# Loading taps and the norm's gain as single rows spread by TensorE, and the first x with its halo in one row a partition

## The chip, the cores and the metric
The kernel runs on one core of a Trainium2 chip. The metric is device time in microseconds (us), the median of repeated runs. The core has five engines with programs of their own: TensorE (PE; PEld are its weight loads), VectorE (DVE), ScalarE (ACT), GpSimd (POOL) and SyncE (SP). SP, ACT and POOL issue transfers (DMA), which 16 shared DMA engines carry out.

## The reference
A causal convolution with 7 taps, one set of taps for each of 8 heads of 24 columns, is followed by a feed-forward block with a layer norm in front and a residual around it. `x` is 8 x 4224 x 192, and x, the taps and g (192 values) are float32; W1 (192 x 768) and W2 (768 x 192) are float64.

```python
w = np.exp(weight - np.max(weight, axis=-1, keepdims=True))     # [8, 7]
w = w / (np.sum(w, axis=-1, keepdims=True) + 1e-09)
x_pad = np.concatenate([zeros(B, 6, D), x], axis=1)
y = einsum('hk,bskhg->bshg', w, x_pad[:, idx].reshape(B, S, K, H, 24))
mu, var = mean(y), mean((y - mu) ** 2)                          # over the 192 columns
yn = (y - mu) / np.sqrt(var + 1e-06) * g_ln
out = y + np.maximum(yn @ w_ch1, 0.0) @ w_ch2
```

## The kernel before
Of each batch entry, 4096 rows are cut into 128 stretches of 32 rows, one stretch to a partition; the last 128 rows of all eight entries make a group of their own. Work goes group by group (`groups`, line 70). The first four groups are small: 6 rows of each stretch of entry 0, then 8 rows a partition of the leftovers, then 10 and 16 rows of entry 0. All later groups have 16. A group needs 6 rows more in front of its own, the halo. For the first group the partition's halo is the end of the stretch of the partition before it, and partition 0's halo is zero.

Per group the convolution runs on VectorE (`conv`, line 402), with the first tap on ScalarE (`first_tap`, line 374). The result y is transposed in 32 x 32 blocks, multiplied by W1 on TensorE (`up`, line 530, or `up_mixed`, line 589; matmuls at line 524), evicted with a ReLU by ScalarE, and multiplied by W2 (`down`, line 730, or `down_fast`, line 781). The mean is taken out by centring W1 once (`centre_w1`, line 326), and g is multiplied into W1's rows. Late groups use sums of quarters of the operands, so as to do fewer products.

The order of the work is written out by hand (`tc.manual_schedule()`); each engine runs its instructions in program order. This is the start, which the change touches:

- ACT issues three loads of g: `ga` (128 partitions, one 4-byte value each, line 192) and twice `gb` (64 partitions each, line 194). SP issues the taps, the same 224 bytes to each of 128 partitions (line 195), then W1 in three loads (lines 198 and 202), then x of the first group (`load_x(0)`: its body at line 163, its halo in two loads at line 165), then x of the second group in eight loads (line 139), then W2 (line 208).
- VectorE and ScalarE turn the taps into softmax weights (lines 255 to 264). ScalarE and POOL then build diagonal matrices of the taps for the last three heads (`tap_matrices`, line 310, and line 305), since the first group's last three heads are convolved on TensorE (`conv_on_pe`, line 315, matmuls at line 320).
- W1 comes as float64 words, which VectorE and ScalarE turn into float32 (`split_words` and `join_words`, lines 218 and 231). Two thirds of W1 go first (`words_a`), with `ga` as a factor at line 245, then the rest (`words_b`) with `gb`. ScalarE's share of `split_words` (lines 221 and 229) stands between two portions of `tap_matrices` (lines 364 to 366).
- TensorE's first work is 20 matmuls on constants whose result nobody reads (`keep_warm(20)`, line 925, matmuls at line 362). They need two constant tiles that POOL makes (lines 285 to 292). After them come the means of W1 (line 329), the first convolution matmuls (320), the rest of the means (332) and the other steps of `centre_w1` (344, 349); ScalarE copies the centred W1 out (354).
- VectorE starts the first group's convolution after `words_b`. W2 is turned into float32 after that.

PSUM is one tile of eight banks. `take_bank` hands them out in turn and `take_set` hands out four neighbours, 0 to 3 or 4 to 7. `carve` cuts short-lived tiles out of the room of the hidden activations. The semaphores that tell of landed loads rotate: a load waits before its issue until the load that used the same semaphore before it has landed. There are eight of them for SP and ACT together.

Of the kernel before, what the change touches and what calls it, by code (L numbers as in the profile page):

```python
# [7 lines left out]
F32 = mybir.dt.float32  # L8
# [3 lines left out]
ALU = mybir.AluOpType  # L12
AX = mybir.AxisListType
# [3 lines left out]
def kernel(  # L17
# [29 lines left out]
    nc = tc.nc  # L47
    PSUM = bass.MemoryType.PSUM
    B, S, D = x.shape
    H, K = weight.shape  # L50
    F = moe_w_ch1.shape[1]
    P = 128
    Q = 64
    C = 32
    GRP = D // H
    PAD = K - 1
    J = 16
    R = 2 * J
# [31 lines left out]
    xr = x[:, 0 : P * R].rearrange("b (p r) d -> b p (r d)", p=P)  # L90
# [12 lines left out]
    consts = ctx.enter_context(tc.tile_pool(name="consts", bufs=1))  # L103
# [15 lines left out]
    def take_bank():  # L119
        i = turn[0] % 8  # L120
        turn[0] = i + 1
        return all_banks[:, i]
# [9 lines left out]
    def load_x(g, queue=nc.sync):  # L132
        b, j0, n = groups[g]
        t = xpool.tile([P, J + PAD, D], F32, tag="xg", name=f"xg{g}")
        xg[g] = t
        flat = t.rearrange("p j d -> p (j d)")
        if b is None:
            for b in range(B):
                queue.dma_start(
                    out=flat[LP * b : LP * b + LP, 0 : (PAD + n) * D],  # L140
                    in_=bass.AP(
                        tensor=x.tensor, offset=(b * S + P * R - PAD) * D,
                        ap=[[n * D, LP], [1, (PAD + n) * D]],
                    ),
                )
            return
        if j0:
            queue.dma_start(
                out=flat[:, 0 : (n + PAD) * D], in_=xr[b, :, (j0 - PAD) * D : (j0 + n) * D]
            )  # L150
            return
        if b:

            queue.dma_start(
                out=flat[:, 0 : (PAD + n) * D],
                in_=bass.AP(
                    tensor=x.tensor, offset=(b * S - PAD) * D, ap=[[R * D, P], [1, (PAD + n) * D]]
                ),
            )
            nc.gpsimd.memset(t[0:1, 0:PAD, :], 0.0)  # L160
            return
        nc.gpsimd.memset(t[0:1, 0:PAD, :], 0.0)
        nc.sync.dma_start(out=flat[:, PAD * D : (PAD + n) * D], in_=xr[b, :, 0 : n * D])
        for p0, p1 in ((16, P), (1, 16)):
            nc.sync.dma_start(
                out=flat[p0:p1, 0 : PAD * D],
                in_=xr[b, p0 - 1 : p1 - 1, (R - PAD) * D : R * D],
            )

    taps = consts.tile([P, H, K], F32, name="taps")
    ga = consts.tile([P, 1], F32, name="ga")
    gb = consts.tile([P, 1], F32, name="gb")

    room = hpool.tile([P, NF * J * P], F32, tag="ht", name="room")
    taken = [0]
# [1 line left out]
    def carve(n, dtype):  # L180
        part = room[:, taken[0] : taken[0] + n].bitcast(dtype)
        taken[0] += n
        return part
# [3 lines left out]
    raw2 = raw2.rearrange("p (n w) -> p n w", w=2)  # L187
    w1_words = moe_w_ch1.bitcast(U32)
    w2_words = moe_w_ch2.bitcast(U32)
    g_col = moe_g_ln.rearrange("(d o) -> d o", o=1)  # L190

    nc.scalar.dma_start(out=ga, in_=g_col[0:P, :])
    for r in range(2):
        nc.scalar.dma_start(out=gb[Q * r : Q * r + Q, :], in_=g_col[P:D, :])
    nc.sync.dma_start(
        out=taps, in_=bass.AP(tensor=weight.tensor, offset=0, ap=[[0, P], [K, H], [1, K]])
    )
    nc.sync.dma_start(
        out=raw1[:, 0:2].rearrange("p s f w -> p (s f w)"), in_=w1_words[0:P, :]
    )  # L200
    for r in range(2):
        nc.sync.dma_start(
            out=raw1[Q * r : Q * r + Q, 2, :, :].rearrange("p f w -> p (f w)"),
            in_=w1_words[P:D, 2 * FH * r : 2 * FH * (r + 1)],
        )
    load_x(0)
    load_x(1)
    nc.sync.dma_start(
        out=raw2.rearrange("p (c d) w -> p c (d w)", d=D),
        in_=w2_words.rearrange("(c p) d -> p c d", p=P),  # L210
# [20 lines left out]
    def join_words(dst, raw, mant, power, g=None):  # L231
# [20 lines left out]
    raw1b = raw1[:, 2]  # L252
    wmax = consts.tile([P, H], F32, name="wmax")
    wsum = consts.tile([P, H], F32, name="wsum")
    nc.vector.tensor_reduce(wmax, taps, axis=AX.X, op=ALU.max)
    nc.vector.tensor_tensor(
        taps, taps, wmax.unsqueeze(2).to_broadcast([P, H, K]), op=ALU.subtract
    )
    nc.scalar.activation(taps, taps, AF.Exp)
    nc.vector.tensor_reduce(wsum, taps, axis=AX.X, op=ALU.add)  # L260
    nc.vector.tensor_scalar(wsum, wsum, scalar1=1e-9, scalar2=None, op0=ALU.add)
    nc.vector.reciprocal(wsum, wsum)
# [23 lines left out]
    for q in range(NQ):  # L286
        m = copy[C * q : C * q + C].rearrange("p (q i) -> p q i", q=NQ)
        nc.gpsimd.affine_select(
            out=m, in_=m, pattern=[[0, NQ], [-1, C]],
# [10 lines left out]
        out=unit, in_=unit, pattern=[[-1, P]], compare_op=ALU.not_equal, fill=1.0, base=0,  # L300
# [5 lines left out]
        out=diag[:, H - 1 - PE_HEADS[0]], in_=taps[:, H - 1, :].unsqueeze(2).to_broadcast([P, K, P]),  # L306
# [642 lines left out]
    for g in range(NG):  # L949
        mixed, last = g in MIXED, g + 1 == NG  # L950
        if g + 2 < NG:
            load_x(g + 2)
# [74 lines left out]
```

## Time and profile before

| what | us |
|---|---|
| median of 3 runs | 966.1 (965.45 to 967.09) |
| profiled execution | 964.65 |
| its span, first to last instruction | 962.8 |
| first tap load to first convolution matmul (line 320) | 0.80 to 16.16 |
| start of the first up-projection (line 524) | 27.35 |
| TensorE busy | 950.3 |
| VectorE busy | 897.2 |

The page of the profile gives busy time by engine, the chain of work that ended last, groups of instructions by source line with their idle time and what ended it, and transfers with their size and the time from issue to landing. The timeline lists instructions in order of time; `x40` says that 40 of one kind are merged, and brackets hold the idle time before the first one and what ended it. A matmul in float32 leaves two records. `room` is the tile that `carve` cuts from, and `ps` is PSUM. The 1.85 us between the profiled execution's time and its span lie before the first instruction or after the last one.

### The profile page before, as it was taken

How to read it: one execution, taken by the hardware profiler on the slowest of the kernel's cores; microseconds unless marked ns; L12 is line 12 of the kernel's file. 1: busy time of each engine (PE TensorE's matmuls, PEld its weight loads, DVE VectorE, ACT ScalarE, POOL GpSimd, SP SyncE). 2: the span in 40 equal slices, each digit the busy share in tenths (PEclk: the TensorE clock that was granted, in tenths of full speed). 3: DMA queues.
4: the chain of work that ended last, by engine and by line, in shares of the span. 5: the costliest groups of instructions: out<-in, count | busy, mean ns of one | idle time of the engine just before them, and what ended most of it. 6: DMA issues, size and time to landing. Idle time of an engine off the chain costs nothing.

```text
span 962.8 us, 38387 instructions
## 1 busy us (share of the span) xinstructions
PE 950.3 (99%) x17274; PEld 717.0 (74%) x17274; DVE 897.2 (93%) x1505; ACT 680.9 (71%) x1097; POOL 249.4 (26%) x383
## 2 busy tenths in 40 slices
PE   7999999999999999999999999999999999999997
PEld 6886586776859677686968778685867868586787
DVE  6999998999999999999999999989989999999867
ACT  5724669586787959687795968778695877866361
POOL 2004411612125131422116131341215221161300
PEclk9999999999999999999999999999999999999999
DMA  8343787769787786969688796968779696766031
GB/s 194 105 125 133 162 212 187 183 130 282 142 243 158 211 189 135 265 133 261 138 237 168 172 240 120 276 140 235 158 179 228 116 282 140 177 138 124 3 68 68
DMA packets 26386, 165.15 MB, mean 172 GB/s; under 512 B 3567, under 2 KB 4463, under 8 KB 18542
## 3 DMA queue, kind: packets, MB, share of 16 engines
q0 software_dynamic: 19120, 99.36, 52.7%
q1 hardware_dynamic: 6798, 63.34, 17.8%
q8 instruction: 135, 2.21, 0.9%
q14 instruction: 29, 0.24, 0.1%
q10 hardware_dynamic: 304, 0.00, 0.0%
HBM read 38.95 MB, written 50.33 MB: 93 GB/s over the span
## 4 chain that ended last, share of the span: by engine, by line
PE 96%; DMA 2%; DVE 2%; issue 0%; DVEq 0%
PE ps L524 48%; PE ps L798 41%; PE ps L745 6%; DMA xg<-in_x_dram 1%; DVE room L765 1%; PE ps L320 1%; DVE room L626 0%; DMA ga<-in_moe_g_ln_dram 0%; PE ps L344 0%; PE ps L349 0%; DVE y L890 0%; PE ps L332 0%; DVE room L774 0%; DVE ot L915 0%; DVE ot L900 0%
## 5 line engine op out<-in xcount | busy, mean ns | idle before, releaser
L408 DVE SCALAR_TENSOR_TENSOR y<-xg,taps,y 128x384 f32<-128x384 f32 (+3 forms) x734 | 367.2, 576 | 1.2 <-ACT y L383 0.5
L798 PE MATMUL ps<-room,w2sums 128*32 128x256 f32 (+1 forms) x4320 | 236.2, 375 | 0.2
L524 PE MATMUL ps<-yt,w 32*128 32x256 f32 (+2 forms) x4104 | 235.6, 379 | 0.1
L620 ACT COPY room<-ps 128x1024 f32<-128x1024 f32 (+1 forms) x132 | 172.0, 1303 | 78.7 <-PE ps L524 78.6
L524 PEld LDWEIGHTS ps<-yt,w 32*128 32x128 f32 x4104 | 204.9, 185 | 26.1 <-issue 9.1
L798 PEld LDWEIGHTS ps<-room,w2sums 128*32 128x32 f32 x4320 | 137.8, 110 | 93.4 <-ACT room L633 5.5
L798 PE MATMUL ps<-room,w 128*32 128x256 f32 (+1 forms) x3240 | 180.5, 375 | 0.1
L765 DVE TENSOR_TENSOR room<-room 128x1024 f32<-128x1024 f32 (+1 forms) x135 | 151.0, 1190 | 6.4 <-PE ps L798 6.4
L798 PEld LDWEIGHTS ps<-room,w 128*32 128x32 f32 x3240 | 103.9, 110 | 69.1 <-DVE room L626 5.2
L524 PE MATMUL ps<-ysums,w1sums 32*128 32x256 f32 x2160 | 125.2, 379 | 0.1
L524 PEld LDWEIGHTS ps<-ysums,w1sums 32*128 32x128 f32 x2160 | 109.0, 185 | 11.2 <-ACT room L620 3.7
L804 ACT COPY cs<-ps 128x256 f32<-128x256 f32 (+1 forms) x180 | 66.4, 370 | 44.1 <-PE ps L798 44.1
L633 ACT ACTIVATE room<-room 128x1024 f32<-128x1024 f32 (+1 forms) x74 | 90.7, 1249 | 8.1 <-DMA room<-parts_cs 7.3
L876 ACT ACTIVATE ot<-ot,r 128x192 f32<-128x192 f32 x232 | 93.8, 462 | 0.0
L883 POOL DMA_DIRECT2D out_dram<-ot x40 | 34.3, 1083 | 201.9 <-ACT ot L876 125.5
L383 ACT ACTIVATE y<-xg,taps 128x384 f32<-128x384 f32 (+3 forms) x141 | 72.8, 611 | 8.1 <-DMA out_dram<-y 6.9
L626 DVE TENSOR_TENSOR room<-room,ps 128x2048 f32<-128x2048 f32 (+1 forms) x20 | 42.5, 2127 | 34.9 <-PE ps L524 34.7
L439 DVE BATCH_NORM_STATS2 st<-y 128x6 f32<-128x192 f32 x264 | 70.2, 343 | 0.0
L524 PE MATMUL ps<-yt,w1sums 32*128 32x256 f32 x1080 | 65.1, 380 | 0.0
L804 ACT COPY room<-ps 128x256 f32<-128x256 f32 (+1 forms) x90 | 33.7, 375 | 44.3 <-PE ps L798 30.9
L524 PE MATMUL ps<-ysums,w 32*128 32x256 f32 x1080 | 64.6, 376 | 0.0
L394 ACT ACTIVATE tb<-xg,taps 128x384 f32<-128x384 f32 x112 | 62.0, 639 | 0.0
(104 smaller groups left out, 880.2 us busy)
## 6 DMA issues: line engine op xcount, KB each, us to landing
xg<-in_x_dram SPq DMA_DIRECT2D x15, 2112.0 KB, 18.1
out_dram<-ot POOLq DMA_DIRECT2D x29, 768.0 KB, 8.7
y<-tb POOLq DMA_DIRECT2D x28, 768.0 KB, 10.7
room<-room POOLq DMA_DIRECT2D x42, 512.0 KB, 5.1
out_dram<-y SPq DMA_DIRECT2D x13, 1536.0 KB, 9.7
room<-parts_cs POOLq DMA_DIRECT2D x14, 1024.0 KB, 7.7
room<-parts_tb POOLq DMA_DIRECT2D x14, 1024.0 KB, 7.5
xg<-in_x_dram SPq DMA_DIRECT2D x1, 1536.0 KB, 7.7
```

The lines of the kernel that those rows point to most:

```text
L383: nc.scalar.mul(y[g][:, 0:n, cs], xg[g][:, 0:n, cs], taps[:, h, 0:1])
L394: nc.scalar.mul(tb[g][:, 0:n, cs], xg[g][:, 1 : 1 + n, cs], taps[:, h, 1:2])
L408: nc.vector.scalar_tensor_tensor(out=y[g][:, 0:n, cs], in0=t[:, k : k + n, cs], scalar=taps[:, h, k : k + 1], in1=y[g][:, 0:n, cs], op0=AL ...
L439: nc.vector.bn_stats(out=sums[g][:, j, :], in_=y[g][:, j, :])
L524: nc.tensor.matmul(banks[:, q, i * w : i * w + w], right[rows, c, P * i : P * i + P], left[rows, :, c, :], start=(first and c == 0 and i = ...
L620: nc.scalar.activation(dst, src, AF.Relu) if relu else nc.scalar.copy(dst, src)
L633: nc.scalar.activation(c, c, AF.Relu)
L745: nc.tensor.matmul(bank[C * q : C * q + C, 0:w], w2[:, f, C * c : C * c + C], left, start=(f == 0), stop=(f == NF - 1),)
L765: nc.vector.tensor_tensor(a[:, *dst, f], a[:, *left, f], a[:, *right, f], op=op)
L798: nc.tensor.matmul(dst[C * q : C * q + C, 0:w], right[:, f, C * c : C * c + C], left[:, f, q], start=(first and f == PAIR), stop=(f == PAI ...
L804: nc.scalar.copy(to[:, c], dst[:, 0:w].rearrange("p (j t) -> p j t", t=t))
L876: nc.scalar.mul(ots[g][:, j, :], ots[g][:, j, :], rstd[g][:, j : j + 1])
```

## The change
The taps and g each come as one row of one partition. A matmul with a row of ones as weights copies the row of taps to all 128 partitions of a PSUM bank. Two more matmuls, each with 128 values of g as weights and a single one as the moving operand, turn g into two columns: its first 128 values, and its last 64 values twice over (for which g's tail is loaded once more behind the row). The softmax of the taps reads PSUM at its first two steps. ScalarE copies the two columns of g out to `gs`, between the taps' exponential and the first `tap_matrices`. The new bank is the first that `take_bank` hands out, and the three matmuls come first in TensorE's program.

The first group's x is no longer loaded as body and halo. Partitions 16 to 127 and partitions 1 to 15 each get one contiguous run of 12 rows (9216 bytes) in one load, and partition 0 gets its 6 own rows in a third. The loads of taps and g move to ACT's queue, three as before; SP's queue has one load less.

```diff
         nc.gpsimd.memset(t[0:1, 0:PAD, :], 0.0)
-        nc.sync.dma_start(out=flat[:, PAD * D : (PAD + n) * D], in_=xr[b, :, 0 : n * D])
         for p0, p1 in ((16, P), (1, 16)):
             nc.sync.dma_start(
-                out=flat[p0:p1, 0 : PAD * D],
-                in_=xr[b, p0 - 1 : p1 - 1, (R - PAD) * D : R * D],
-            )
+                out=flat[p0:p1, 0 : (PAD + n) * D],
+                in_=bass.AP(
+                    tensor=x.tensor, offset=(b * S + p0 * R - PAD) * D,
+                    ap=[[R * D, p1 - p0], [1, (PAD + n) * D]],
+                ),
+            )
+        nc.sync.dma_start(out=flat[0:1, PAD * D : (PAD + n) * D], in_=xr[b, 0:1, 0 : n * D])
...
-    ga = consts.tile([P, 1], F32, name="ga")
-    gb = consts.tile([P, 1], F32, name="gb")
+    gs = consts.tile([P, 2], F32, name="gs")
+    ga, gb = gs[:, 0:1], gs[:, 1:2]
...
-    g_col = moe_g_ln.rearrange("(d o) -> d o", o=1)
-
-    nc.scalar.dma_start(out=ga, in_=g_col[0:P, :])
+    row, ones = carve(H * K + 2 * P, F32)[0:1], carve(P, F32)[0:1]
+    g_row = row[:, H * K :]
+    nc.scalar.dma_start(out=row[:, 0 : H * K], in_=weight.rearrange("(o h) k -> o (h k)", o=1))
+    g_in = moe_g_ln.rearrange("(o d) -> o d", o=1)
+    nc.scalar.dma_start(out=g_row[:, 0:D], in_=g_in)
+    nc.scalar.dma_start(out=g_row[:, D : 2 * P], in_=g_in[:, P:D])
+    nc.vector.memset(ones, 1.0)
+    spread = take_bank()
+    nc.tensor.matmul(spread[:, 0 : H * K], ones, row[:, 0 : H * K], start=True, stop=True)
     for r in range(2):
-        nc.scalar.dma_start(out=gb[Q * r : Q * r + Q, :], in_=g_col[P:D, :])
-    nc.sync.dma_start(
-        out=taps, in_=bass.AP(tensor=weight.tensor, offset=0, ap=[[0, P], [K, H], [1, K]])
-    )
+        nc.tensor.matmul(
+            spread[:, H * K + r : H * K + r + 1], g_row[:, P * r : P * r + P], ones[:, 0:1],
+            start=True, stop=True,
+        )
+    raw_taps = spread[:, 0 : H * K].rearrange("p (h k) -> p h k", k=K)
...
-    nc.vector.tensor_reduce(wmax, taps, axis=AX.X, op=ALU.max)
+    nc.vector.tensor_reduce(wmax, raw_taps, axis=AX.X, op=ALU.max)
     nc.vector.tensor_tensor(
-        taps, taps, wmax.unsqueeze(2).to_broadcast([P, H, K]), op=ALU.subtract
+        taps, raw_taps, wmax.unsqueeze(2).to_broadcast([P, H, K]), op=ALU.subtract
     )
     nc.scalar.activation(taps, taps, AF.Exp)
+    nc.scalar.copy(gs, spread[:, H * K : H * K + 2])
```

## The prediction
> **What bounds the kernel now.** I read the engine shares and the chain that ended last on the page first, then the chain of the first 80 us in order of time, then the timeline of the first 50 us, then the waits.
>
> The page, engine shares:
> ```profile
> span 962.8 us, 38387 instructions
> ...
> PE 950.3 (99%) x17274; PEld 717.0 (74%) x17274; DVE 897.2 (93%) x1505; ACT 680.9 (71%) x1097; POOL 249.4 (26%) x383
> ```
> TensorE is busy for 99%. By stages it is busy 779.8 of the 780.0 us from 120 to 900 us, so nothing the change touches can be gained there. What can move is when TensorE's unbroken stream starts. The chain of the first 80 us (start, length, what):
> ```profile
> 0.80 4.46 DMA ga<-in_moe_g_ln_dram
> ...
> 5.27 10.80 DMA xg<-in_x_dram
> ...
> 16.16 1.95 PE ps L320 x14
> ...
> 27.35 13.13 PE ps L524 x285
> ...
> 52.32 15.75 PE ps L524 x288
> ```
> It says that g's first load releases the halo of x, the halo releases the first convolution matmul at 16.16, and from 27.35 on TensorE doesn't stop. I don't take the first arrow at its word. The halo's issue did wait for `ga` (a semaphore in rotation), but it was issued at 5.27 while the body of x, issued at 2.92, landed only at 13.0: the rings were full, and the wait cost nothing.
>
> The timeline, what sets 16.16:
> ```profile
> 4.88 7.68 PE L362 MATMUL ps<-room 128*128 128x128 f32 x40 [4.88 <-POOL room L292]
> ...
> 5.11 0.21 DVE L255 TENSOR_REDUCE wmax<-taps 128x8 f32<-128x56 f32 x1 [4.18 <-DMA taps<-in_weight_dram]
> ...
> 6.90 1.86 ACT L313 ACTIVATE room<-room,taps 128x128 f32<-128x128 f32 x6 [1.04 <-DVE taps L263]
> ...
> 8.68 0.56 DVE L220 TENSOR_SCALAR room<-room 128x768 uint32<-128x768 uint32 x1 [1.88 <-DMA room<-in_moe_w_ch_dram]
> ...
> 13.37 1.56 PE L329 MATMUL ps<-room 128*128 128x384 f32 x4 [0.81 <-DVE room L245]
> ...
> 15.52 0.62 DVE L245 SCALAR_TENSOR_TENSOR room<-room,gb 128x384 f32<-128x384 f32 x1
> ...
> 16.16 1.95 PE L320 MATMUL ps<-xg,room 128*128 128x144 f32 x14 [1.24 <-DMA xg<-in_x_dram]
> ...
> 16.60 6.81 DVE L408 SCALAR_TENSOR_TENSOR y<-xg,taps,y 128x144 f32<-128x144 f32 x24 [0.46 <-ACT y L383]
> ```
> Three things arrive together. x is complete at 16.07. VectorE is done with W1 at 15.52+0.62=16.14. TensorE has been free since 14.92. TensorE idles 0.81 us before L329 and 1.24 us before L320: 2.05 us to be had from it, no more. The keep-warm matmuls (L362) end at 12.56 and are covered today, because L329 waits for W1 until 13.37.
>
> The page and the first 60 us, transfers (KB each, us to landing):
> ```profile
> xg<-in_x_dram SPq DMA_DIRECT2D x1, 576.0 KB, 10.1
> ...
> room<-in_moe_w_ch_dram SPq DMA_DIRECT2D x2, 192.0 KB, 8.3
> ...
> gb<-in_moe_g_ln_dram ACTq DMA_DIRECT2D x2, 0.2 KB, 8.1
> ...
> ga<-in_moe_g_ln_dram ACTq DMA_DIRECT2D x1, 0.5 KB, 4.5
> ```
> Each 256-byte copy of `gb` takes about 8.1 us. The last one lands at 10.31.
>
> **What the Trainium skill says.** "DMA: Bandwidth & Descriptors", section Queues, rings and completion order: each engine takes turns between the queues that have work, a packet of descriptors at a time. The trace agrees, more coarsely: in its packet records the earliest engine writes the completion of W1's first load at 5.39 and its first `gb` packet starts at 5.40. A small load on ACT's queue waits for a whole transfer of SP's. The section Why a DMA increments its semaphore by 16 and not by 1 says that the slowest dimension fixes how many engines are used (127 rows: one; 112: sixteen; 15: fifteen). It fits the split of x at partition 16; no row here shows 127. "TensorE: Matmul & The Clock Gate", Part 1 (The HAM clock gate): the clock rises after a whole busy window of a free-running 3.4 us grid. Here the keep-warm records stand 0.213 us apart up to 11.0 us and 0.112 after, 6.1 us after their start. With the page's grid that delay is 3.4 to 6.8 us, so the 40 records take an estimated 6.1 to 7.7 us, middle 6.9.
>
> **The change, part by part.**
>
> *Loads.* The taps' 128 packets of 224 B, all from one address, start from 1.96 to 4.74; eight engines have them by 3.31, the other eight land up to 5.09. This lag of some 2 us stays with those engines up to x (body 10.33 to 13.0, halo 12.35 to 16.07). Without them W1's first load starts on all engines at about 2.0 (issue 0.80 instead of 1.24, first packet 1.16 after the first issue now). 48 KB an engine at the 22 GB/s that the records show (seven 6144 B packets from 3.77 to 5.74) is 2.2 us, plus a first latency: done at 4.5, not 8.65. Its two halves take 1.35 us each at most on the earliest engine now (5.43 to 6.77), 0.9 if faster: 6.3 to 7.2.
>
> *x.* The same 1147 KB in half as many packets. At 233 GB/s (the mean of the slices from 4.5 to 16.1 us) 4.9 us: landed at about 12, 15 if the lag of the engines had another cause. Not slower by the larger packets: 1536 KB of 12288 B landed in 7.7 us, latency included. SP issues one load fewer, so what follows is issued 0.44 earlier; POOL's program is not passed by anything. The one-row rest waits for the taps' row to land before it is issued (the semaphores rotate over eight loads), which the full rings hide; with empty rings it would cost one small landing, about 2 us. The second group's x follows, and W2's load behind it (26.65 now, needed at 27.30) moves with them.
>
> *Spread.* Three row loads on ACT's queue (three issues, as now), a memset (L216's kind, 0.06), three small matmuls, a PSUM reduce in L255's place (0.21). The taps' chain from landing to finished taps is 5.09 to 6.80 = 1.7 us; add 0.5 for the matmul (the first keep-warm record took 0.58 cold). These matmuls stand **ahead of the keep-warm matmuls** in TensorE's program, and the new copy of g on ACT stands ahead of L313. So both now wait for the landing G of the last piece of g. TensorE: keep-warm starts at G+0.4 (two records 0.21 apart), not at 4.88. ACT: L313 starts at G+0.75 (0.4, and a copy of L324's kind, 0.28), not at 6.90.
>
> *G.* By turns: if the taps' row gets ahead of W1's first load, g's two pieces come after W1's first load and its first half: 5.8 to 6.3. If it doesn't, they come a half later: 6.7 to 7.5. Bounds: nothing queued ahead, 3.8 (third issue at about 1.8, 1.16 to the first packet, some 0.8 to land); as late as `gb` now, 10.31. I take 6.7.
>
> *The sum on TensorE.* Keep-warm 7.1 to 14.0. L329 at 14.0. W1's first part is ready for it earlier, at 13.35: L313 starts at 7.45, its six take 1.80 until L221 may start, L221 to L245 takes 3.03 (9.27 to 12.30), L245 to L329 1.07. L320 1.40 later (13.37 to 14.76 is when it could have started now): 15.4, x being there since 12. Against 16.16 this is 0.76 earlier. One `take_bank` more shifts the banks by one: the first up-projection needs ScalarE's copies 2 to 5 of L354 instead of 3 to 6, 0.37 apart, so 0.37 earlier. Together 1.1 us.
>
> *VectorE beside it.* from L221's start to the end of W1 it is 6.87 (9.27 to 16.14), so W1 is done at 7.45+1.80+6.87=16.1, and the convolution starts there, 0.5 before today's 16.60 (ScalarE's first taps, free of x's wait, are then done before). It may lag TensorE by its idle 0.82 before L234 of W2 and by 0.3 (transposed at 51.95, L524 at 52.25); 0.5+1.1=1.6 covers the 1.1. After 68 us the reserve is about 10 us.
>
> The profiled execution took 964.65 with a span of 962.8; the median is 966.1. A gain of 1.1 makes the span 961.7 and the median **965.0**. A measurement can tell about 0.2%, 1.9 us; the forecast lies inside.
>
> **Rivals.**
> *All of it arrives (963.7).* g lands by 5.3, or the clock rises early: L329 at its covered 12.6, all 2.05 us of TensorE's idle time and the 0.37 are won: 2.4. For it: 2.05 us of idle time exist, and the rows are a few packets. Against: today's `gb` alternates with W1. From G=5.9 on (at the middle clock) the gain is under 1.9.
> *Keep-warm behind g (968.4, slower).* One mechanism: the last piece of g still lands about as late as `gb` now (10.1). Keep-warm 10.5 to 17.4, L320 18.8, 2.6 late, less 0.37: 2.3 lost. It decides from G=7.8 on (16.53 less 1.4, 6.9 and 0.4), by 0.2% from G=9.8. For it: the 8.1 us of `gb`. Against: W1 and its halves start some 2 us earlier.
> *Nothing arrives (966.3).* The lag of eight engines isn't the taps' doing. Then W1's first load lands only its 0.44 earlier, at 8.2, g's last piece with it at about 8.0, keep-warm ends at 15.3, and L320 starts at 16.7: 0.5 late, less 0.37. For it: the lag shows in `ga` too (3.03 to 5.26). Against: `ga` also reads one small address range, and later loads show no lagging half.
>
> **How the numbers follow.** Forecast 0.46, all arrives 0.31, slower 0.11, nothing 0.12. Faster by over 0.2%: 0.31 and 0.05 of the forecast's early edge, 0.36; slower: 0.10 (0.01 of the rival stays under 0.2%); within: 0.54. The range takes the full gain with run-to-run play (963.5), and at the other end G=8.3 with the slow clock: 966.9. The forecast's own range is 964.2 to 966.0 (G 5.9 to 7.5).
>
> **What would show it.** Right: L362 starts at 6.5 to 7.5, released by a matmul that waited for a g load; no idle time before L320 from x; x landed by 13; TensorE idle before L329 small; L524 at 26.0 to 26.5 and its second block some 1.1 us before 52.32. Wrong: L362 still at 4.9 (the full gain); x landing after 15 (the lag isn't the taps'); L362 after 8 (slower); the copy of g waiting on ACT beyond 8.3 with VectorE, not TensorE, late at L524; or a gain of L524 at 27.35 that is gone at 52.32.

## The result and the profile after

The median after is 965.7 us (964.37 to 967.42 over 22 runs), against 967.33 us (965.24 to 970.3 over 22 runs) of the kernel before, run beside it on the same chip. The ratio is 0.9981, with a 95% interval of 0.9973 to 0.9989: 1.84 us faster by the ratio. The interval leaves out 1, so the kernel is faster, but the gain stays just under the 0.2% (1.9 us) that the forecast took as the least a measurement can tell. The forecast was a gain of 1.1 us, and the range 963.5 to 966.9 holds the time.

The page of the kernel after, engine shares:
```profile
span 962.9 us, 38399 instructions
...
PE 950.6 (99%) x17280; PEld 716.5 (74%) x17280; DVE 897.8 (93%) x1506; ACT 681.0 (71%) x1098; POOL 249.8 (26%) x383
```
The profiled execution took 964.68 us. Its span is 962.9 us and that of before was 962.8, so the two pages show no gain at all while the medians do. One reason is the execution that was profiled before: its 964.65 us are less than any of the other 22 times of that kernel. A second profiled execution of the unchanged kernel, shown below, starts its stream 3.9 us later. The gain has to be looked for against that one too.

The timeline of the kernel after, start in us, length, engine and line, out<-in, and in brackets the idle time before it and what ended it:
```profile
2.14 0.64 PE L203 MATMUL ps<-room 1*128 1x56 f32 x2 [2.14 <-DMA room<-in_weight_dram]
...
6.72 0.58 PE L205 MATMUL ps<-room 1*128 1x1 f32 x2 [0.38 <-DMA room<-in_moe_g_ln_dram]
...
7.24 6.50 PE L376 MATMUL ps<-room 128*128 128x128 f32 x40
7.34 0.22 DVE L268 TENSOR_REDUCE wmax<-ps 128x8 f32<-128x56 f32 x1 [6.29 <-PE ps L205]
...
8.00 0.14 ACT L273 COPY gs<-ps 128x2 f32<-128x2 f32 x1
...
9.13 1.86 ACT L327 ACTIVATE room<-room,taps 128x128 f32<-128x128 f32 x6 [0.99 <-DVE taps L277]
...
14.70 1.56 PE L343 MATMUL ps<-room 128*128 128x384 f32 x4 [0.96 <-DVE room L258]
...
16.09 1.88 PE L334 MATMUL ps<-xg,room 128*128 128x144 f32 x14
...
16.85 0.62 DVE L258 SCALAR_TENSOR_TENSOR room<-room,gs 128x384 f32<-128x384 f32 x1
17.39 6.78 DVE L422 SCALAR_TENSOR_TENSOR y<-xg,taps,y 128x144 f32<-128x144 f32 x24
```
(L203 and L205 are the new matmuls, L376 is the keep-warm of the old L362, L343 and L334 are the old L329 and L320, L268 the old L255, L327 the old L313, L258 the old L245, L422 the old L408.) The row of taps is spread at 2.14, but VectorE's reduce of it waits until 7.34, and the releaser is not the spread of the taps (L203). It is the spread of g (L205). The tap matrices therefore start at 9.13, later than the 6.90 of before, and VectorE ends W1 at 17.47 and starts its convolution at 17.39, 0.8 later than before.

The chain that ended last, first 80 us of the kernel after (start, length, what):
```profile
1.58 5.10 DMA room<-in_moe_g_ln_dram
...
7.34 0.23 DVE wmax L268
...
9.13 1.86 ACT room L327 x6
...
14.70 1.56 PE ps L343 x4
16.25 1.72 PE ps L334 x14
```
Where the chain of before ran through x, it now runs through the last piece of g, the softmax of the taps, the tap matrices and W1. x is not in it.

The transfers of the first 60 us, kernel after (KB each, us from issue to landing):
```profile
xg<-in_x_dram SPq DMA_DIRECT2D x1, 1008.0 KB, 12.2
...
room<-in_moe_w_ch_dram SPq DMA_DIRECT2D x1, 768.0 KB, 5.9
...
xg<-in_x_dram SPq DMA_DIRECT2D x1, 135.0 KB, 12.4
```
W1's first load was issued at 0.80 and landed at 6.7 (8.65 before): the first of the 16 engines had its share at 4.4, the eighth at 4.9, the last at 6.7. The two loads of x were issued from 2.46 on; the second landed at 15.4.

TensorE's timeline where the stream begins, kernel after:
```profile
27.00 5.13 PE L538 MATMUL ps<-yt,w 32*128 32x192 f32 x96
32.29 8.43 PE L538 MATMUL ps<-yt,w 32*128 32x192 f32 x192 [0.15 <-ACT room L528]
40.65 11.91 PE L759 MATMUL ps<-room,w 128*32 128x192 f32 x288
52.48 1.79 PE L538 MATMUL ps<-yt,w 32*128 32x256 f32 x28
```
The same of the kernel before:
```profile
40.41 11.91 PE L745 MATMUL ps<-room,w 128*32 128x192 f32 x288
52.25 2.01 PE L524 MATMUL ps<-yt,w 32*128 32x256 f32 x32
```
A lead of 0.35 us at the first up-projection (27.00 against 27.35) is 0.23 us of lag at the second. It is lost within the first block, where ScalarE empties the PSUM banks (`room L528`) only after its share of W2's conversion, and VectorE, later than before, starts W2 at 28.07 instead of 27.30:
```profile
30.28 1.26 ACT L242 ACTIVATE spare<-spare,low 128x1152 int32<-128x1152 int32 x1 [0.16 <-DVE spare L239]
31.44 0.79 ACT L528 ACTIVATE room<-ps 128x768 f32<-128x768 f32 x1
```

### The profile page after: what moved, and what is told of

Read it like the earlier page. It is cut to its first block, busy times and chain, and to the rows that moved or that the text cites. A ratio compares the mean times of both kernels' runs of the same rounds, so it can differ in the third digit from the quotient of the medians.

```text
span 962.9 us, 38399 instructions
## 1 busy us (share of the span) xinstructions
PE 950.6 (99%) x17280; PEld 716.5 (74%) x17280; DVE 897.8 (93%) x1506; ACT 681.0 (71%) x1098; POOL 249.8 (26%) x383
## 4 chain that ended last, share of the span: by engine, by line
PE 96%; DVE 2%; DMA 1%; ACT 1%; issue 0%; ACTq 0%; DVEq 0%
PE ps L538 48%; PE ps L812 41%; PE ps L759 6%; DVE room L779 1%; PE ps L334 1%; DMA room<-in_moe_g_ln_dram 1%; DVE room L640 0%; DMA out_dram<-y 0%; ACT room L327 0%; PE ps L358 0%; DVE y L904 0%; PE ps L343 0%; ACT w L368 0%; PE ps L363 0%; PE ps L346 0%
## 5 line engine op out<-in xcount | busy, mean ns | idle before, releaser
L422 DVE SCALAR_TENSOR_TENSOR y<-xg,taps,y 128x384 f32<-128x384 f32 (+3 forms) x734 | 367.2, 577 | 0.2
L538 PEld LDWEIGHTS ps<-yt,w 32*128 32x128 f32 x4104 | 204.9, 185 | 26.5 <-issue 9.6
L408 ACT ACTIVATE tb<-xg,taps 128x384 f32<-128x384 f32 x112 | 61.8, 633 | 0.0
```

The lines of the kernel that those rows point to most:

```text
L408: nc.scalar.mul(tb[g][:, 0:n, cs], xg[g][:, 1 : 1 + n, cs], taps[:, h, 1:2])
L422: nc.vector.scalar_tensor_tensor(out=y[g][:, 0:n, cs], in0=t[:, k : k + n, cs], scalar=taps[:, h, k : k + 1], in1=y[g][:, 0:n, cs], op0=AL ...
L538: nc.tensor.matmul(banks[:, q, i * w : i * w + w], right[rows, c, P * i : P * i + P], left[rows, :, c, :], start=(first and c == 0 and i = ...
```

## The experiments

The theory after the result: the repeated read of the 224 bytes of taps delays half of the DMA engines; to be rid of it is worth several microseconds, and the change gives most of that back by what it makes wait for g. The rivals: the gain comes from the new load of x, or from fewer transfers in general, or there is nothing to be had beyond what the change shows. Where a number of DMA packets, of single engines or of the TensorE clock is given without a line of a view, it was read from the trace's own records. Times are medians; each ratio is to the kernel before run beside it, with its 95% interval.

### The two parts alone
`rows_only`: the kernel after, with x loaded as before.
```diff
+        nc.sync.dma_start(out=flat[:, PAD * D : (PAD + n) * D], in_=xr[b, :, 0 : n * D])
         for p0, p1 in ((16, P), (1, 16)):
             nc.sync.dma_start(
-                out=flat[p0:p1, 0 : (PAD + n) * D],
+                out=flat[p0:p1, 0 : PAD * D],
+                in_=xr[b, p0 - 1 : p1 - 1, (R - PAD) * D : R * D],
...
-        nc.sync.dma_start(out=flat[0:1, PAD * D : (PAD + n) * D], in_=xr[b, 0:1, 0 : n * D])
```


> Taps and g as rows, x of the first group still as body and halo. Theory (the broadcast load of the taps and the 256 four-byte loads of g make half of the DMA engines late, and without them W1 and x land earlier and more evenly): W1's first load lands at about 6.7 us as with the whole change, x by about 15, VectorE's first convolution at about 17.4 because it waits behind g; time 1.2 to 2.0 us under the kernel before, as the whole change. Rival (the half as many and larger packets of x bring the gain): the time is that of the kernel before within 0.5 us.

Measured: 965.46 us, 0.9976 (0.9967 to 0.9986), as the whole change within the intervals. `x_only` is the reverse, the kernel before with the new load of x:
```diff
-        nc.sync.dma_start(out=flat[:, PAD * D : (PAD + n) * D], in_=xr[b, :, 0 : n * D])
         for p0, p1 in ((16, P), (1, 16)):
             nc.sync.dma_start(
-                out=flat[p0:p1, 0 : PAD * D],
-                in_=xr[b, p0 - 1 : p1 - 1, (R - PAD) * D : R * D],
+                out=flat[p0:p1, 0 : (PAD + n) * D],
...
+        nc.sync.dma_start(out=flat[0:1, PAD * D : (PAD + n) * D], in_=xr[b, 0:1, 0 : n * D])
```


> Only the x load of the first group is changed; taps and g are loaded as in the kernel before. Theory (the gain is in the small loads): W1's first load lands at 8.2 to 8.7 us, x at about 16, the first convolution matmul within 0.3 us of 16.16, time within 0.5 us of the kernel before. Rival (the larger packets of x bring the gain): x lands 1 to 2 us earlier and the time is 1.2 to 2.0 us under the kernel before.

Measured: 969.22 us, 1.0018 (1.0009 to 1.0027): 1.7 us slower. Its timeline:
```profile
9.75 0.56 DVE L223 TENSOR_SCALAR room<-room 128x768 uint32<-128x768 uint32 x1 [2.76 <-DMA room<-in_moe_w_ch_dram]
...
19.28 2.88 PE L323 MATMUL ps<-xg,room 128*128 128x144 f32 x14 [3.27 <-DMA xg<-in_x_dram]
```
x is complete only at 19.2 and TensorE idles 3.27 us for it. Neither the theory (the time of the kernel before) nor the rival (a gain) foresaw a loss. The gain comes from the rows, and the load of x with its halo in one row a partition is no help: alone it costs.

### How the kernel before starts another time
`before_2` is the kernel before, with no edit, profiled again.


> The kernel before, unchanged, once more. Its profiled execution (964.65 us) lies under nearly all of its other executions (965.2 to 970.6), so its start may not be the usual one. Theory (the usual start is later because x lands later): this execution takes 966 to 969 us, x lands after 17, the first convolution matmul starts at 17 to 20 and TensorE's clock may drop once while it waits. Rival (the start is always as on the first page, and the rest differs): the first convolution matmul at 16.0 to 16.4, and the time is lost after 60 us.

Measured: 968.21 us in one execution, with a span of 966.5. Its timeline:
```profile
5.23 0.21 DVE L255 TENSOR_REDUCE wmax<-taps 128x8 f32<-128x56 f32 x1 [4.30 <-DMA taps<-in_weight_dram]
...
9.65 0.56 DVE L220 TENSOR_SCALAR room<-room 128x768 uint32<-128x768 uint32 x1 [2.74 <-DMA room<-in_moe_w_ch_dram]
...
18.38 2.57 PE L320 MATMUL ps<-xg,room 128*128 128x144 f32 x14 [2.47 <-DMA xg<-in_x_dram]
...
20.74 2.56 PE L332 MATMUL ps<-room 128*128 128x384 f32 x4
...
31.25 13.14 PE L524 MATMUL ps<-yt,w 32*128 32x192 f32 x288
```
The taps land as late as on the page of before (5.2), W1 a microsecond later (9.6) and x 2.2 us later (18.3). W1's first packet starts at 3.76 instead of 2.52, so here all sixteen engines are late and not eight. The four matmuls of L332 take 2.56 us; the page of before has
```profile
17.95 1.46 PE L332 MATMUL ps<-room 128*128 128x384 f32 x4
```
From 19.6 to 23.0 the trace's clock record stands at half rate. The Trainium skill, "TensorE: Matmul & The Clock Gate", Part 1, says that the clock falls after an idle window of about 3.4 us. The half rate lasts 3.4 us, which agrees; the idle stretch was shorter, 2.47 us, and in the last 3.4 us before the fall TensorE had worked for 1.2. The first up-projection starts 3.9 us after that of the page of before, and the span is 3.7 us longer. The idle stretch before the stream is thus paid twice, as waiting and as an estimated 1.7 us (half of 3.4) of slower work.

This start is frequent, but not the rule. The granted clock is on record for 82 more executions of the kernel before, on three chips. In 30 it is as low as here (0.997 or less), and their median is 968.6 us; the other 52 have 966.9. None of the 22 executions of the kernel after is below 0.998. Why W1 and x come later in one execution than in another no run shows.

### The repeated read
Two runs test what makes the engines late. `taps_distinct` keeps the load of the taps as it was, 128 packets of 224 bytes, but reads each from another address (the first values of each partition's x, so it computes with other taps):
```diff
-        out=taps, in_=bass.AP(tensor=weight.tensor, offset=0, ap=[[0, P], [K, H], [1, K]])
+        out=taps, in_=bass.AP(tensor=x.tensor, offset=0, ap=[[R * D, P], [K, H], [1, K]])
```


> The kernel before, but each partition's 224 bytes of taps are read from a place of their own (the first values of its stretch of x) instead of all from the same 224 bytes: as many packets of the same size, other values, so the output is not the reference's. Theory (the load is slow because all its packets read one place): the taps land by 3.5 us on all engines instead of 5.1, W1's first load by 7.0 instead of 8.65, and the time is 1 to 2 us under the kernel before. Rival (the count of small packets, or the start of the engines, makes the lag): taps at 4.5 to 5.3, W1's first load after 8, time within 0.6 us of the kernel before.

`taps_row` reads the taps once, as one row on SP's queue, and spreads them with one matmul. g and x are loaded as in the kernel before.
```diff
-    nc.sync.dma_start(
-        out=taps, in_=bass.AP(tensor=weight.tensor, offset=0, ap=[[0, P], [K, H], [1, K]])
-    )
+    row, ones = carve(H * K, F32)[0:1], carve(P, F32)[0:1]
+    nc.sync.dma_start(out=row, in_=weight.rearrange("(o h) k -> o (h k)", o=1))
+    nc.vector.memset(ones, 1.0)
+    spread = take_bank()
+    nc.tensor.matmul(spread[:, 0 : H * K], ones, row, start=True, stop=True)
+    raw_taps = spread[:, 0 : H * K].rearrange("p (h k) -> p h k", k=K)
...
-    nc.vector.tensor_reduce(wmax, taps, axis=AX.X, op=ALU.max)
+    nc.vector.tensor_reduce(wmax, raw_taps, axis=AX.X, op=ALU.max)
     nc.vector.tensor_tensor(
-        taps, taps, wmax.unsqueeze(2).to_broadcast([P, H, K]), op=ALU.subtract
+        taps, raw_taps, wmax.unsqueeze(2).to_broadcast([P, H, K]), op=ALU.subtract
     )
```


> The kernel before with the taps alone loaded as one row and spread by TensorE; g still comes in 256 loads of four bytes, x as before. Theory (the taps' 128 packets make the lag): W1's first load lands at 6.5 to 7.2 us, the last piece of g at 8 to 9, x by 15.5, and the time is 1.5 to 2.5 us under the kernel before, as with both. Rival (g's 256 four-byte packets make it): W1's first load after 8, time within 0.7 us of the kernel before.

Measured: `taps_distinct` 962.34 us, 0.9952 (0.9939 to 0.9966); `taps_row` 961.92 us, 0.9950 (0.9938 to 0.9962), some 4.8 us faster than before and the lowest ratio of the study; its interval lies clear of that of the whole change (0.9973 to 0.9989). Both gain more than was expected (1 to 2 and 1.5 to 2.5 us). The timeline of `taps_distinct`:
```profile
2.83 0.21 DVE L255 TENSOR_REDUCE wmax<-taps 128x8 f32<-128x56 f32 x1 [1.90 <-DMA taps<-in_x_dram]
...
6.54 0.56 DVE L220 TENSOR_SCALAR room<-room 128x768 uint32<-128x768 uint32 x1 [1.45 <-DMA room<-in_moe_w_ch_dram]
...
13.33 1.95 PE L320 MATMUL ps<-xg,room 128*128 128x144 f32 x14 [0.54 <-DMA xg<-in_x_dram]
...
24.52 13.14 PE L524 MATMUL ps<-yt,w 32*128 32x192 f32 x288
```
And that of `taps_row`:
```profile
2.85 0.22 DVE L258 TENSOR_REDUCE wmax<-ps 128x8 f32<-128x56 f32 x1 [1.78 <-PE ps L199]
...
6.01 0.71 DVE L223 TENSOR_SCALAR room<-room 128x768 uint32<-128x768 uint32 x1 [1.11 <-DMA room<-in_moe_w_ch_dram]
...
13.49 1.95 PE L323 MATMUL ps<-xg,room 128*128 128x144 f32 x14
...
24.48 13.34 PE L527 MATMUL ps<-yt,w 32*128 32x192 f32 x288
```
With as many packets of the same size from distinct places, the taps are in by 2.8 instead of 5.1; W1 follows at 6.5 instead of 8.7 to 9.6, and x at 13.3 instead of 16.1 to 18.3. `taps_distinct` also reads another tensor, but `taps_row` reads the old one, once, and comes to the same figures. What the two share is that nothing is read 128 times over. So the 128 reads of one place were the cause, not the number of packets. Nor were it g's loads: `taps_row` keeps all 256 packets of 4 bytes. Why such reads are slow no run shows.

### What the spread of g takes back
`g_bank` is the kernel after with g's two matmuls in another PSUM bank than the taps:
```diff
+    g_bank = all_banks[:, 7]
     for r in range(2):
         nc.tensor.matmul(
-            spread[:, H * K + r : H * K + r + 1], g_row[:, P * r : P * r + P], ones[:, 0:1],
+            g_bank[:, r : r + 1], g_row[:, P * r : P * r + P], ones[:, 0:1],
             start=True, stop=True,
         )
...
-    nc.scalar.copy(gs, spread[:, H * K : H * K + 2])
+    nc.scalar.copy(gs, g_bank[:, 0:2])
```


> The whole change, but the two g columns are made in a PSUM bank of their own (one that is not used until later), so that the taps' reduce has no write of g in its bank. Theory (the reduce waits for the last piece of g only because both lie in one bank): the reduce starts at about 2.9 us instead of 7.34, the first tap matrices at 7.4 to 7.6 instead of 9.13 (ScalarE's copy of g still stands ahead of them), VectorE's first convolution at 16.0 to 16.3 instead of 17.39; keep-warm still at 7.2; time 0.3 to 1.0 us under the whole change. Rival (it waits for the order of the matmuls, not the bank, or VectorE's lateness costs nothing): reduce still at 7.3, or the time is that of the whole change.

Measured: 964.73 us, 0.9969 (0.9956 to 0.9981), beside 0.9981 (0.9973 to 0.9989) of the whole change: lower, but the intervals overlap. Its timeline:
```profile
2.82 0.22 DVE L269 TENSOR_REDUCE wmax<-ps 128x8 f32<-128x56 f32 x1 [1.77 <-PE ps L203]
...
7.49 0.16 ACT L274 COPY gs<-ps 128x2 f32<-128x2 f32 x1 [3.91 <-PE ps L206]
...
15.16 1.88 PE L335 MATMUL ps<-xg,room 128*128 128x144 f32 x14
...
15.81 6.78 DVE L423 SCALAR_TENSOR_TENSOR y<-xg,taps,y 128x144 f32<-128x144 f32 x24
```
The reduce now runs at 2.82, right behind the taps' own matmul, instead of at 7.34. The order of the matmuls is as it was, so the bank alone made it wait 4.5 us for g. The Trainium skill, "PSUM — Partial Sum Buffer", section PSUM bank collisions raise a hardware error, says that the compiler's scheduler adds a dependency between any two instructions on different engines that touch the same bank and 32-partition quadrant, reads and writes alike. That agrees with the wait seen here, between a read of columns 0 to 55 and a write of columns 56 and 57; it is a wait that the program was given, and no run shows what would happen without it. The convolution starts 1.6 us earlier on VectorE and 0.9 on TensorE. What stays is the wait of ScalarE's copy of g (3.91), ahead of the tap matrices, and the keep-warm behind g.

`g_later` takes those away as well: g's matmuls go into the keep-warm, behind its first 8, and the copy of g behind ScalarE's first share of W1. (Not shown below: the bank of the keep-warm is taken once, ahead of both parts.)
```diff
-    for r in range(2):
-        nc.tensor.matmul(
-            spread[:, H * K + r : H * K + r + 1], g_row[:, P * r : P * r + P], ones[:, 0:1],
-            start=True, stop=True,
-        )
...
-    nc.scalar.copy(gs, spread[:, H * K : H * K + 2])
...
     split_words(*words_a)
+    keep_warm(8)
+    g_bank = all_banks[:, 7]
+    for r in range(2):
+        nc.tensor.matmul(
+            g_bank[:, r : r + 1], g_row[:, P * r : P * r + P], ones[:, 0:1],
+            start=True, stop=True,
+        )
+    nc.scalar.copy(gs, g_bank[:, 0:2])
     tap_matrices(range(3, K))
...
-    keep_warm(20)
+    keep_warm(12)
```


> As the g bank of its own, and the two g matmuls stand behind the first 8 keep-warm matmuls, ScalarE's copy of g behind its first share of the W1 split. Nothing early waits for g any more. Theory (waits on g hold TensorE and ScalarE back): keep-warm starts at 4.9, the tap matrices at about 4.5, W1's first part is ready by 11.5 to 12.5, the first means at about 12.8 (end of keep-warm); then only the landing of x (13 to 15.5) holds the first convolution matmul; time 0.7 to 1.6 us under the whole change. Rival (x is what holds the start, so the waits on g are covered): within 0.4 us of the whole change.

Measured: 964.72 us, 0.9974 (0.9964 to 0.9984). In its trace the first convolution matmul is at 14.29 and the first up-projection at 25.28, 0.8 us before `g_bank`, and TensorE waits 0.69 us for x there, as the theory had it. Yet the time isn't below that of `g_bank`. The lead is gone later on; this is taken up below.

`later_old_x` and `bank_old_x` are `g_later` and `g_bank` with x loaded as before, so all that remains of the change is the rows. Both differ from their partner by the same lines:
```diff
+        nc.sync.dma_start(out=flat[:, PAD * D : (PAD + n) * D], in_=xr[b, :, 0 : n * D])
         for p0, p1 in ((16, P), (1, 16)):
             nc.sync.dma_start(
-                out=flat[p0:p1, 0 : (PAD + n) * D],
+                out=flat[p0:p1, 0 : PAD * D],
+                in_=xr[b, p0 - 1 : p1 - 1, (R - PAD) * D : R * D],
...
-        nc.sync.dma_start(out=flat[0:1, PAD * D : (PAD + n) * D], in_=xr[b, 0:1, 0 : n * D])
```


> The rows for taps and g with g's matmuls behind the first 8 keep-warm matmuls and in a bank of their own, and x of the first group loaded as body and halo as in the kernel before. Theory (contiguous rows of x with the halo land about 1 us later than body and halo apart): x at 13.0 to 13.8, the first convolution matmul at 13.3 to 13.9, the first up-projection at about 24.4, time 3.0 to 3.8 us under the kernel before and 0.3 to 1.0 under the same with the new x load. Rival (an early lead is given back later, whatever it is): start as said, but the time within 0.3 us of the same with the new x load (ratio 0.9974).

> The rows for taps and g with g's columns in a bank of their own, keep-warm and ScalarE still behind g, x as body and halo as before. Theory (keep-warm behind g holds the start there, not x): the first convolution matmul at 15.0 to 15.4 as with the new x load (15.16), time within 0.6 us of it (ratio 0.9963 to 0.9975), that is 1.5 us or more over the taps row alone. Rival (the new x load is what costs): 1 us or more under the same with the new x load (ratio under 0.996).

Measured: `later_old_x` 964.6 us, 0.9963 (0.9949 to 0.9978); `bank_old_x` 964.2 us, 0.9964 (0.9952 to 0.9976). Neither differs from its partner with the new x by more than the intervals. Both stand above the 0.9950 (0.9938 to 0.9962) of `taps_row`, though the intervals overlap, and both start later than was expected: 15.25 instead of 13.3 to 13.9, and 16.74 instead of 15.0 to 15.4. The timeline of `later_old_x` shows one reason:
```profile
4.89 3.78 PE L368 MATMUL ps<-room 128*128 128x128 f32 x16 [2.11 <-POOL room L297]
...
8.60 1.01 PE L375 MATMUL ps<-room 1*128 1x1 f32 x4
9.54 4.58 PE L368 MATMUL ps<-room 128*128 128x128 f32 x24
...
15.25 1.88 PE L325 MATMUL ps<-xg,room 128*128 128x144 f32 x14
```
The keep-warm is cut in two by g's matmuls, and its records halve their distance only at 13.0, 8.1 us after its start; on the page of before it was 6.1. The keep-warm ends at 14.1 and the means of W1 and the convolution queue behind it, while x had been there since 13.9. In `g_later` the same order got the full rate at 9.1. So that the cut is what made it late is a reading, not shown. In `bank_old_x` g came later than in `g_bank`: the keep-warm starts at 7.97 and the means of W1 behind it at 15.45 (7.38 and 13.87 in `g_bank`), and TensorE doesn't wait for x. So the keep-warm does hold the start there, as its theory said, but later. From the first keep-warm matmul to the full rate it took, by the clock records, 3.0 to 6.2 us in the other thirteen traces, so a single start can differ by a microsecond or more for this alone.

### The price of a keep-warm behind g
`warm_behind_g` is `taps_row` with one tiny matmul that reads `gb` ahead of the keep-warm, so only TensorE waits for g, neither the taps nor ScalarE.
```diff
         idle = take_bank()
+        nc.tensor.matmul(idle[:, 0:1], less, gb, start=True, stop=True)
         for _ in range(times):
             nc.tensor.matmul(idle[:, 0:P], less, copy, start=True, stop=True)
```


> The taps row alone, and one small matmul on g's second column tile ahead of the keep-warm matmuls, so that TensorE starts them only when the last piece of g has landed (8.2 us there); nothing else waits for g. Theory (keep-warm behind g is a cost of its own in the whole change): keep-warm at 8.3 to 8.7 and over at 14.5 to 16.2, the first means then, the first convolution matmul at 16 to 17.6 instead of 13.49, time 2.0 to 4.0 us over the taps row alone. Rival (TensorE catches up, VectorE sets the start): the first up-projection within 0.5 us of 24.48 and time within 0.6 us of the taps row alone.

Measured: 964.1 us, 0.9962 (0.9949 to 0.9975). Its timeline:
```profile
7.54 0.55 PE L364 MATMUL ps<-gb,room 128*128 128x1 f32 x2 [4.73 <-DMA gb<-in_moe_g_ln_dram]
7.95 7.49 PE L366 MATMUL ps<-room 128*128 128x128 f32 x40
...
16.57 1.88 PE L323 MATMUL ps<-xg,room 128*128 128x144 f32 x14
...
27.48 13.33 PE L528 MATMUL ps<-yt,w 32*128 32x192 f32 x288
```
Everything else is early (VectorE's convolution starts at 13.99), and TensorE, with 40 matmuls that nobody reads, is late: 16.57 against 13.49 and 27.48 against 24.48 in `taps_row`. The profiled span is 963.18 against 961.2. The ratios, taken on two chips, are 0.9962 against 0.9950 and their intervals overlap. So the start is 3.0 us later, shown; the price in time is some 1 to 2 us by the ratios and the spans, less than the 2.0 to 4.0 expected and not clear of the noise.

### The load of x, once more
`taps_row_new_x` is `taps_row` with the new load of x:
```diff
-        nc.sync.dma_start(out=flat[:, PAD * D : (PAD + n) * D], in_=xr[b, :, 0 : n * D])
         for p0, p1 in ((16, P), (1, 16)):
             nc.sync.dma_start(
-                out=flat[p0:p1, 0 : PAD * D],
-                in_=xr[b, p0 - 1 : p1 - 1, (R - PAD) * D : R * D],
+                out=flat[p0:p1, 0 : (PAD + n) * D],
...
+        nc.sync.dma_start(out=flat[0:1, PAD * D : (PAD + n) * D], in_=xr[b, 0:1, 0 : n * D])
```


> The taps alone as one row, g in its columns as before, and the new x load of the change (whole rows of 12, partition 0 apart). Theory (the new x load lands about 1 us later, and x is what holds the first convolution matmul once the taps are a row): x complete at 14.2 to 15 us instead of 13.40, the first convolution matmul 0.8 to 1.6 us later than 13.49, time 0.7 to 1.7 us over the taps row alone (ratio to the kernel before 0.9955 to 0.9968). Rival (the new x load makes no difference once the engines start together): within 0.4 us of the taps row alone (0.9946 to 0.9954).

Measured: 963.39 us, 0.9959 (0.9948 to 0.9970). Its timeline:
```profile
14.52 1.95 PE L326 MATMUL ps<-xg,room 128*128 128x144 f32 x14 [1.33 <-DMA xg<-in_x_dram]
```
With the rest out of the way x is what TensorE waits for, 1.33 us, and it is complete 1.0 later than in `taps_row` (14.4 against 13.4), although the load ahead of it, W1's last, landed at 8.6 to 8.7 in both. The packets of 9216 bytes took 0.55 us each (median), those of 4608 bytes in `taps_row` 0.22. Whether the length of the rows, the overlap of what neighbouring partitions read or the third load is the reason isn't separated. In time the intervals of the two overlap; only `x_only` shows by itself, outside its interval, that this part costs.

`taps_row_act` asks whether the row of taps is better issued first on ACT's queue, which frees SP for W1 0.4 us earlier:
```diff
+    row, ones = carve(H * K, F32)[0:1], carve(P, F32)[0:1]
+    nc.scalar.dma_start(out=row, in_=weight.rearrange("(o h) k -> o (h k)", o=1))
     nc.scalar.dma_start(out=ga, in_=g_col[0:P, :])
...
-    row, ones = carve(H * K, F32)[0:1], carve(P, F32)[0:1]
-    nc.sync.dma_start(out=row, in_=weight.rearrange("(o h) k -> o (h k)", o=1))
```


> The taps alone as one row, issued first on ACT's queue instead of SP's, so that W1's first load is issued 0.41 us earlier; g and x as before. Theory (the loads now run one behind another, and x is what holds the start): W1 and x land 0.3 to 0.5 us earlier than in the taps row alone (x at 12.9 to 13.1), time 0.2 to 0.5 us under it (ratio 0.9945 to 0.9948 to the kernel before). Rival (the end of keep-warm or VectorE's W1 holds it): within 0.15 us of the taps row alone.

Measured: 962.77 us, 0.9951 (0.9933 to 0.9969). No gain: W1 starts to be split at 6.04 (6.01 in `taps_row`), and the first convolution matmul comes at 14.08 instead of 13.49. That theory failed. The trace shows one reason: the last load of x was issued only at 6.03 (3.94 in `taps_row`), when W1's first load had landed at 6.01, since in the new order the two share a semaphore, and x was complete at 13.95 instead of 13.4.

### How much of an early start reaches the end
The table has the start of the first up-projection and the span of fourteen profiled executions.

| kernel | first convolution matmul | first up-projection | span |
|---|---|---|---|
| taps_row | 13.49 | 24.48 | 961.2 |
| taps_distinct | 13.33 | 24.52 | 959.9 |
| taps_row_act | 14.08 | 25.07 | 960.9 |
| g_later | 14.29 | 25.28 | 962.9 |
| taps_row_new_x | 14.52 | 25.51 | 961.9 |
| g_bank | 15.16 | 26.08 | 963.0 |
| later_old_x | 15.25 | 26.16 | 963.4 |
| after | 16.09 | 27.00 | 962.9 |
| rows_only | 16.19 | 27.10 | 962.7 |
| before | 16.16 | 27.35 | 962.8 |
| warm_behind_g | 16.57 | 27.48 | 963.2 |
| bank_old_x | 16.74 | 27.65 | 964.5 |
| before_2 | 18.38 | 31.25 | 966.5 |
| x_only | 19.28 | 32.15 | 966.3 |

A straight line through the fourteen pairs has a slope of 0.74 (standard error 0.09), and the spans lie about it with a standard deviation of 0.7 us. So a start that is 1 us earlier goes with about three quarters of it, and a single execution tells little below 1 us. The four kernels with g in a bank of its own all lie 0.65 to 1.1 us above the line and none of the others more than 0.3; what they lose later isn't explained. With the medians the link is looser: `g_later` starts at 25.28 and has 0.9974, `warm_behind_g` at 27.48 and has 0.9962.

A lead is lost in two places. In the first block `taps_row_new_x`, 1.84 us ahead of the page of before, keeps 0.51: VectorE waits 1.64 us for W2, and TensorE then 1.00 us for ScalarE's first eviction. Between 538 and 734 us `g_later` goes from 1.3 us ahead to none. In that stretch before and after wait for VectorE. The chain that ended last, of before and then of after:
```profile
718.45 3.46 DVE room L765 x3
```
```profile
718.44 3.47 DVE room L779 x3
```
These two come to the same half-sum on VectorE at the same time, though after was 0.4 us behind at 566 us. It isn't a fixed time for all: at 734 us `taps_distinct` is still 2.9 us ahead of the page of before, and `before_2` 3.7 us behind. In `g_later`, 1.6 and 1.8 us ahead of them at the second block, the stretch shows gaps of TensorE instead, the longest this one, with no releaser in the trace:
```profile
669.58 0.78 issue
```
What fixes the pace of that stretch was not tried and stays open.

## Why the prediction was right or wrong

The number held: forecast 965.0 and a gain of 1.1, measured 965.7 and 1.84. The working did not hold throughout; two errors of opposite sign met (Spread and The base, below), so that it held is in part luck. Of the signs of being right two came: the keep-warm starts at 7.24 behind g, and TensorE doesn't idle for x. Three did not: x landed at 15.4 and not by 13, TensorE idles 0.96 us before L329, and the up-projection starts at 27.00 and not at 26.0 to 26.5.

- **Loads.** The mechanism was right: the repeated read of the taps was what made eight engines late (`taps_distinct`). The rival *Nothing arrives* falls with it. The size was off: W1's first load was put at 4.5 and landed at 6.7 (6.3 in `g_bank`, 6.0 in `taps_row`). The rate came from one engine's packets, and for the first engine 4.5 is about right (it had its share at 4.4); the last came 2.3 us after it.
- **G.** Predicted 6.7, measured 6.68, but by luck. The 6.7 stood for W1's first load at 4.5 and at least one of its halves ahead of g. In the trace g landed with that first load (6.69) and ahead of the halves (7.60 and 8.84): the load was 2.2 us later, and the halves did not come in between.
- **The sum on TensorE, keep-warm.** Predicted 7.1 to 14.0; measured 7.24 to 13.74. That the keep-warm stands behind g makes the start later, as `warm_behind_g` shows, and the forecast had it.
- **Spread, the step that failed.** It put the first tap matrices at G plus 0.75, as if only the copy of g stood between them and g. It took for granted that the taps' softmax would run at the taps' own landing. The softmax reads the bank that g's matmuls write, so all of its 1.7 us comes after G: 9.13, which is G plus 2.45. From there the rest of the working carries on to within 0.4 us: W1 done at 17.47 instead of 16.1, L329 at 14.70 instead of 14.0, L320 at 16.09 instead of 15.4. `g_bank`, where this one wait is gone, has L320's like at 15.16 and the convolution on VectorE at 15.81, close to the forecast of 15.4 and 16.1.
- **x.** Predicted at about 12, "not slower by the larger packets". It landed at 15.4, and in one row a partition it is slower, not equal: 14.4 against 13.4 where nothing else differs (`taps_row_new_x`). A landing after 15 was to show that the lag isn't the taps'; it came for another reason. In the kernel after this is hidden, since W1 is later still; `rows_only` gives the same time.
- **Bank shift.** Predicted 0.37. From the first convolution matmul to the first up-projection it is 10.91 in after and 11.19 on the page of before: 0.28. Little of it stays: in the first block the kernels with the extra bank lose 0.2 us or more against the page of before, while those without it (`before_2`, `x_only`, `taps_distinct`) lose none. No run moves the bank alone.
- **VectorE beside it.** Its lateness was to be covered by its idle 0.82 us and 0.3 of slack. It was 0.8 late where it should have been 0.5 early, and TensorE's lead of 0.35 at the first up-projection was gone at the second block. The prediction had named that very sign. What it lacked is the way: not VectorE's transposes at the second block, but ScalarE's evictions in the first, which stand behind its share of W2.
- **The base.** The sum was made against one profiled execution and carried over to the median. That execution was the earliest of all: the span was forecast at 961.7 and came to 962.9, no less than before, while the median was hit. In `before_2` TensorE waits 2.47 us for x and then works 3.4 us at half rate, so that there was more to be had than the 2.05 us of idle time counted. More than a third of the 82 executions before had so low a clock, and none of the 22 after. Against the others (966.9) the gain is an estimated 1.2 us, which leaves the rest of the 1.84 to such starts.
- **Rivals.** *All of it arrives* would have needed g by 5.3; it came at 6.68. *Keep-warm behind g* would have needed g after 7.8.

## What to carry to other kernels

Don't read one small place 128 times to fill 128 partitions: read it once and spread it by a matmul, and do this alone. Give data that lands at another time its own PSUM bank and its own place in the queues, for a bank shared with a late arrival makes the early one wait; here that shows in the starts, and not clear of the noise in the time. Profile the kernel before twice when the expected gain is about as large as the play of its start.

## What the runs showed of the hardware that was not expected

- 128 packets of 224 bytes from one address landed at 5.1 to 5.2 us, from 128 addresses at 2.8 us; the lag carried on to W1 and x behind them and was worth 4.6 us of the kernel's time. g's 256 packets of 4 bytes, at different addresses, did no such harm.
- A read of one part of a PSUM bank was held 4.5 us behind a matmul into another part of it (7.34 against 2.82 with two banks).
- x in rows of 9216 bytes was complete 1.0 us later than the same data in rows of 4608 bytes (14.4 against 13.4); a packet took 0.55 us against 0.22.
- 2.5 to 3.3 us of waiting on TensorE brought 3.4 us at half rate (19.6 to 23.0 in `before_2`, 20.1 to 23.6 in `x_only`); 1.33 us in `taps_row_new_x` brought none.
- The full rate of TensorE came 3.0 to 6.2 us after the first keep-warm matmul in thirteen traces, and 8.1 us after it in `later_old_x`.
